# Decode attention with a Mish layer: wo loaded in runs of 32 KB, w1 read at unit step, the output made and stored as four rows

## The chip, the cores and the metric

The kernel runs on one core of a Trainium2 chip. A core has TensorE (matmuls into PSUM), VectorE, ScalarE, GpSimd, and SyncE (SP), which here issues most of the transfers; 16 DMA engines move data between the chip's memory and the core's 128-partition SBUF. The metric is the device time of one execution in microseconds. Three runs of the kernel before gave a median of 1329.84 us.

## The reference

One token (x of 512 elements) passes through an attention layer with a long cache and then a dense layer, each behind a layernorm and with its input added to its output. All tensors are bf16.

```python
# x (1,1,512); caches (1,32,32768,128); wq (512,4096); wo (4096,512)
# w1 (512,1376); b1 (1376); w2 (1376,512)
q = (layernorm(x) @ wq), as 32 heads of 128
scores = einsum("bhqd,bhkd->bhqk", q, k_cache) * 128 ** -0.5
o = einsum("bhqk,bhkd->bhqd", softmax(scores), v_cache)
h = x + o.reshape(1, 1, 4096) @ wo
g = layernorm(h) @ w1 + b1
out = h + (g * tanh(softplus(g))) @ w2
```

Each of the 32 heads reads 8 MB of keys and 8 MB of values, so the two caches are 512 MiB of the 548 MB that the kernel reads.

## The kernel before, in words

**A ring of six slots.** `ring` is a buffer of six slots, each 128 partitions x 32 KB, 4 MB in all. Everything large passes through it in the order of the list `order` (lines 186 to 193): wq, then the keys and values in halves of a head. The keys of head t + 1 alternate with the values of head t. After the values of head 30 come wo, then `w12` (w1 and w2 in one slot), then the two halves of the values of head 31. SP walks through this list (lines 231 to 255). Before an item it waits until the item six places earlier has been used up (line 234), and then it issues the transfers. The last item, the second half of head 31's values, is issued in four pieces of 64, 32, 16 and 16 tiles (`TAIL`), each with a semaphore of its own, so that work can begin on the first piece.

A half of keys or values is one transfer of 128 rows of 32 KB. wo is one transfer of 128 partitions x 32 heads x 1 KB (line 239): partition k receives, for each head h, row 128 h + k of wo. w1 is 128 rows of 11,008 B (line 241), w2 is 128 rows of 10,240 B and one last group of 96 rows of 1 KB (lines 242 and 243). Rows that are neighbours in memory lie in one partition: partition p holds rows 4p to 4p + 3 of w1.

**A half of keys** is 128 tiles of 128 x 128. TensorE transposes eight of them into PSUM (line 340), VectorE copies them to SBUF (line 343), and TensorE multiplies each by the query of the head (line 313). **A half of values** is 128 products of a tile with a column of probabilities, added up in PSUM (line 365). Between them stands the softmax of a head (lines 378 to 397). `oev` (line 373) divides a head's sum by its total and writes it as a column of `oT`.

**The end.** `project(h)` (line 431) multiplies the column of head h by the four column groups of wo. Here column group c holds the output elements 4m + c, m from 0 to 127, so `wo_v[:, h, c, :]` steps over four elements. Heads 0 to 30 are projected before the values of head 31 are used, head 31 after them. Then `lnh1` (line 445) adds x, `layernorm(1)` follows (lines 280 to 290), and 44 products make the hidden layer from w1 (line 457). Hidden element 10m + j stands in partition m of column j, so the weights step over ten elements; the last 96 hidden elements have a column of their own. The bias was put into the same PSUM columns earlier, by a product with the identity (line 439). Eight small steps make the activation (lines 461 to 467), 44 products with w2 make the output as a column of 128 x 4 (line 472), VectorE adds h (line 475), and SP stores 128 rows of 8 B (line 256).

**Order of work.** Each engine runs its own list in the order in which the program calls `S.step` for it; a step waits for the named steps of other engines. A transfer adds 16 to its semaphore, and `ready_wait` (line 201) gives the count at which an item has landed.

**The start.** x is loaded on ScalarE's queue (line 261) as 128 rows of 8 B and cast by VectorE (line 274); the two parts of b1 are loaded on GpSimd's queue (lines 266 and 268).

Of the kernel before, what the change touches and what calls it, by code (L numbers as in the profile page):

```python
# [6 lines left out]
BF16 = mybir.dt.bfloat16  # L7
F32 = mybir.dt.float32
I32 = mybir.dt.int32
ALU = mybir.AluOpType  # L10
# [3 lines left out]
PE, ACT, DVE, POOL, SP = "pe", "act", "dve", "pool", "sp"  # L14
# [81 lines left out]
def build_kernel(nc, A_x, A_k_cache, A_v_cache, A_wq, A_wo, B_w1, B_b1, B_w2, out):  # L96
    D = A_x.shape[-1]
    Dh = 128
    HD = A_wq.shape[1]
    H = HD // Dh  # L100
    Sk = A_k_cache.shape[2]
    F = B_w1.shape[1]
    KC = D // 128
# [5 lines left out]
    NS = 6  # L109
    TPS = 128  # L110
    SLOT = TPS * Dh
# [6 lines left out]
    FJ = F // 128  # L118
    FLAST = F - FJ * 128
    W1 = KC * F  # L120
    assert HALVES == 2 and KC == 4 and H <= 32 and FLAST > 0
    assert KC * HD == SLOT and H * D == SLOT
    assert W1 + (FJ + 1) * D <= SLOT

    allocs = []

    def sb(shape, dt, name):
        cm = nc.sbuf_tensor(name, shape, dt)
        t = cm.__enter__()
        allocs.append(cm)  # L130
        return t.ap()
# [7 lines left out]
    ring = sb([128, NS, SLOT], BF16, "ring")  # L139
# [3 lines left out]
    oT = sb([128, H], BF16, "oT")  # L143
# [3 lines left out]
    rtotc = sb([128, H], F32, "rtotc")  # L147
    gmax = sb([1, H], F32, "gmax")
    identi = sb([128, 128], I32, "identi")
    ident = sb([128, 128], F32, "ident")  # L150
    identb = sb([128, 128], BF16, "identb")
    onesm = sb([128, 128], F32, "onesmat")
    meanm = sb([128, 128], F32, "meanmat")
    epsc = sb([128, 1], F32, "epsc")
    xb = sb([128, KC], BF16, "xb")
    b1b = sb([128, FJ + 1], BF16, "b1b")
    b1f = sb([128, FJ + 1], F32, "b1f")
    lnx = sb([128, 2, 2, KC], F32, "lnx")
    lns = sb([128, 2, 8], F32, "lns")
    xnT = sb([128, 2, KC], BF16, "xnT")  # L160
    hsb = sb([128, 6, FJ + 1], F32, "hsb")
    actT = sb([128, FJ + 1], BF16, "actT")
    outT = sb([128, KC], BF16, "outT")

# [10 lines left out]
    hid_ps = S_b[0][:, 0:FJ + 1]  # L175
    y2_ps = S_b[1][:, 0:KC]

# [20 lines left out]
    def slot_of(what):  # L198
        return where[what] % NS

    def ready_wait(what):
        i = where[what]
        return (ready[i % NS], 16 * (i // NS + 1 + (2 if i % NS == where[("w12",)] % NS and i >= where[("w12",)] else 0)))

# [6 lines left out]
    wq_v = ring[:, slot_of(("wq",)), :].rearrange("p (k n) -> p k n", k=KC)  # L211
    wo_v = ring[:, slot_of(("wo",)), :].rearrange("p (h m c) -> p h c m", h=H, c=KC)
    w12 = ring[:, slot_of(("w12",)), :]
    w1_v = w12[:, 0:W1].rearrange("p (k n) -> p k n", k=KC)
    w2_v = w12[:, W1:W1 + FJ * D].rearrange("p (j m c) -> p j c m", j=FJ, c=KC)
    w2t_v = w12[0:FLAST, W1 + FJ * D:W1 + (FJ + 1) * D].rearrange("p (m c) -> p c m", c=KC)

    events = {}

    def program(S):  # L220
# [7 lines left out]
        def start(dst, src, s):  # L228
            S.dma(SP, lambda: sp.dma_start(dst, src).then_inc(s, 16))  # L229

        for i, what in enumerate(order):
            slot = i % NS
            if i >= NS:
                S.wait(SP, [free_name(order[i - NS])])
            flat = ring[:, slot, :]
            if what[0] == "wq":
                start(flat, A_wq.rearrange("(p k) n -> p (k n)", k=KC), ready[slot])
            elif what[0] == "wo":
                start(flat.rearrange("p (h n) -> p h n", h=H), A_wo.rearrange("(h k) n -> k h n", k=Dh), ready[slot])
            elif what[0] == "w12":  # L240
                start(w12[:, 0:W1], B_w1.rearrange("(p k) n -> p (k n)", k=KC), ready[slot])
                start(w12[:, W1:W1 + FJ * D], B_w2[0:FJ * 128, :].rearrange("(p j) n -> p (j n)", j=FJ), ready[slot])
                start(w12[0:FLAST, W1 + FJ * D:W1 + (FJ + 1) * D], B_w2[FJ * 128:F, :], ready[slot])
            else:
                kind, h, half = what
                cache = A_k_cache if kind == "k" else A_v_cache
                rows = cache[0, h, half * 128 * TPS:(half + 1) * 128 * TPS, :].rearrange("(p r) d -> p (r d)", r=TPS)
                if what == order[-1]:
                    at = 0
                    for n, s in zip(TAIL, piece_sems):  # L250
                        start(flat[:, at * Dh:(at + n) * Dh], rows[:, at * Dh:(at + n) * Dh], s)
                        at += n
                    assert at == TPS
                else:
                    start(flat, rows, ready[slot])
        S.dma(SP, lambda: sp.dma_start(out[0, 0, :].rearrange("(p c) -> p c", c=KC), outT[:, :]).then_inc(s_out, 16),
              waits=["fin"])
        S.wait(SP, [(s_out, 16)])


        S.dma(ACT, lambda: a.dma_start(xb[:, :], A_x[0, 0, :].rearrange("(p c) -> p c", c=KC)).then_inc(s_x, 16))
        if S.emit and S.only == ACT:
            a.preload_act_table_set("natural_log_exp_and_others")
        S.step(POOL, lambda: g.iota(identi[:, :], [[-1, 128]], base=0, channel_multiplier=1), name="iota")
        S.step(POOL, lambda: g.memset(b1b[:, :], 0.0), name="b1z")
        S.dma(POOL, lambda: g.dma_start(b1b[:, 0:FJ], B_b1[0:FJ * 128].rearrange("(p j) -> p j", j=FJ)).then_inc(s_b1, 16),
              waits=["b1z"])
        S.dma(POOL, lambda: g.dma_start(b1b[0:FLAST, FJ:FJ + 1], B_b1[FJ * 128:F].rearrange("(p o) -> p o", o=1)).then_inc(s_b1, 16))
        S.step(DVE, lambda: v.memset(onesm[:, :], 1.0), name="consts0")
# [3 lines left out]
        S.step(DVE, lambda: v.tensor_copy(identb[:, :], ident[:, :]), name="identb", waits=["ident"])  # L273
        S.step(DVE, lambda: v.tensor_copy(lnx[:, 0, 0, :], xb[:, :]), name="lnh0", waits=[(s_x, 16)])  # L274

# [96 lines left out]
        def oev(h):  # L372
            S.step(DVE, lambda: v.tensor_tensor(oT[:, h:h + 1], o_ps[:, h % 2:h % 2 + 1], rtotc[:, h:h + 1], ALU.mult),  # L373
                   name=f"oev{h}", waits=[f"pv{h}", f"rcp{h}"])

# [48 lines left out]

        def project(h):
            for c in range(KC):
                last = h == H - 1 and c == KC - 1
                waits = []
                if c == 0:
                    waits = [f"oev{h}"] + ([ready_wait(("wo",))] if h == 0 else [])  # L430
                S.step(PE, lambda c=c: t_.matmul(yps[:, c:c + 1], wo_v[:, h, c, :], oT[:, h:h + 1],  # L431
                                                 start=(h == 0 and c == 0), stop=last, skip_group_check=True),
                       name=("y" if last else None), waits=waits)

        for h in range(H - 1):
            project(h)
        soft_c(H - 1)
        S.step(DVE, lambda: v.tensor_copy(b1f[:, :], b1b[:, :]), name="b1f", waits=[(s_b1, 32)])
        S.step(PE, lambda: t_.matmul(hid_ps, ident[:, :], b1f[:, :], start=True, stop=False, skip_group_check=True),
               waits=["b1f", f"exp{H - 2}", f"exp{H - 1}"])  # L440
        pv(H - 1, 0, 0, TPS)
        pv(H - 1, 1, 0, TPS)
        oev(H - 1)
        project(H - 1)
        S.step(DVE, lambda: v.tensor_tensor(lnx[:, 1, 0, :], yps[:, 0:KC], lnx[:, 0, 0, :], ALU.add), name="lnh1", waits=["y"])
        layernorm(1)


        for j in range(FJ + 1):
            for kc in range(KC):  # L450
                if j < FJ:
                    w = w1_v[:, kc, 0:FJ * 128].rearrange("p (m j) -> p j m", j=FJ)[:, j, :]
                else:
                    w = w1_v[:, kc, FJ * 128:F]
                W = 128 if j < FJ else FLAST
                last = j == FJ and kc == KC - 1
                S.step(PE, lambda w=w, W=W, j=j, kc=kc, last=last: t_.matmul(  # L457
                    hid_ps[0:W, j:j + 1], w, xnT[:, 1, kc:kc + 1], start=False, stop=last, skip_group_check=True),
                    name=("hid" if last else None), waits=(["xn1", ready_wait(("w12",))] if j == 0 and kc == 0 else ()))
# [7 lines left out]
        S.step(DVE, lambda: v.tensor_tensor(actT[:, :], hid_ps, tt, ALU.mult), name="act", waits=["tt"])  # L467
        for c in range(KC):
            for j in range(FJ + 1):
                w = w2_v[:, j, c, :] if j < FJ else w2t_v[:, c, :]  # L470
                W = 128 if j < FJ else FLAST
                S.step(PE, lambda w=w, W=W, j=j, c=c: t_.matmul(y2_ps[:, c:c + 1], w, actT[0:W, j:j + 1],  # L472
                                                                start=(j == 0), stop=(j == FJ)),
                       name=("y2" if c == KC - 1 and j == FJ else None), waits=(["act"] if c == 0 and j == 0 else ()))
        S.step(DVE, lambda: v.tensor_tensor(outT[:, :], y2_ps, lnx[:, 1, 0, :], ALU.add), name="fin", waits=["y2"])

# [44 lines left out]
```

## Time and profile before

| what | us |
|---|---|
| median of three runs (lowest to highest) | 1329.84 (1328.77 to 1330.07) |
| the profiled execution, whole | 1330.19 |
| the span of its profile | 1328.4 |
| TensorE matmuls, busy | 1106.9 |
| VectorE, busy | 721.7 |
| ScalarE, busy | 20.6 |
| issue to landing, a half of keys (median) | 39.6 |
| issue to landing, wo | 43.5 |
| issue to landing, w1 | 39.1 |
| issue to landing, w2 without its last group | 9.2 |
| issue to landing, the output | 3.2 |

The span goes from the first to the last instruction of one profiled execution; its whole time is 1.8 us more. The mean granted clock of TensorE is 0.755 of full speed. Busy times of engines overlap. "Issue to landing" starts when SP issues a transfer, and holds the time behind other transfers in the queue. L343 and the like are lines of the kernel before.

### The profile page before, as it was taken

Reading aid. Unit: us, or ns where it says so; the run is one execution under the profiler, and the core shown is the slowest. Engines: PE = TensorE matmul, PEld = TensorE weight load, DVE = VectorE, ACT = ScalarE, POOL = GpSimd, SP = SyncE. Lnnn points to the kernel's source line nnn. Section 1 sums busy time; section 2 is a strip of 40 time slices with the busy share of each in tenths; the row PEclk is TensorE's granted clock in tenths of the full one; section 3 lists DMA queues with packets and bytes.
Section 4 is the critical chain, followed back from the end, with each engine's and each line's share of the span. In section 5 each row is a group of like instructions: output and inputs, shape, how many; then the busy total and the mean of one; then the engine's idle time right before and its main releaser. Section 6 shows DMA issues by size and latency. Waiting matters only on the chain.

```text
span 1328.4 us, 51752 instructions
## 1 busy us (share of the span) xinstructions
PE 1106.9 (83%) x25118; PEld 1073.6 (81%) x25118; DVE 721.7 (54%) x1210; ACT 20.6 (2%) x70; POOL 1.7 (0%) x8
## 2 busy tenths in 40 slices
PE   3887888988888988889889888888888988887984
PEld 3887887888887988888878888788887988887884
DVE  2754655655655654646556556556556555645540
ACT  0000000000000000000000000000000000000000
POOL 0000000000000000000000000000000000000000
PEclk9877868777878777667778667777778677768775
DMA  9999999999999999999999999999999999999974
GB/s 389 429 429 426 432 426 425 433 426 428 431 424 432 427 426 432 425 425 434 426 428 429 425 425 422 424 427 417 428 425 428 425 427 425 426 411 431 383 281 195
DMA packets 24080, 551.40 MB, mean 415 GB/s; under 512 B 2528, under 2 KB 6720, under 8 KB 6976
## 3 DMA queue, kind: packets, MB, share of 16 engines
q1 hardware_dynamic: 23664, 548.09, 96.9%
q8 instruction: 196, 3.21, 1.0%
q14 instruction: 12, 0.10, 0.0%
q10 hardware_dynamic: 144, 0.00, 0.0%
q0 software_dynamic: 64, 0.00, 0.0%
HBM read 548.08 MB, written 0.00 MB: 413 GB/s over the span
## 4 chain that ended last, share of the span: by engine, by line
PE 75%; issue 13%; DVE 8%; DMA 4%; SPq 0%; ACT 0%
PE tps L340 43%; PE ops L365 16%; PE sps L313 12%; DVE ering L343 7%; DMA ring<-in_A_v_cache_dram 2%; DMA ring<-in_A_k_cache_dram 2%; PE hlp L387 1%; PE hlp L382 1%; PE hlp L395 1%; PE sps L457 0%; SPq L229 0%; PE sps L472 0%; PE hlp L282 0%; DVE pmax L378 0%; ACT lns L287 0%
## 5 line engine op out<-in xcount | busy, mean ns | idle before, releaser
L343 DVE COPY ering<-tps 128x1024 bf16<-128x1024 bf16 x1024 | 681.7, 692 | 368.9 <-PE tps L340 365.9
L340 PE MATMUL tps<-identb,ring 128*128 128x128 bf16 x8192 | 755.7, 248 | 35.4 <-issue 31.7
L340 PEld LDWEIGHTS tps<-identb,ring 128*128 128x128 bf16 x8192 | 583.2, 112 | 42.6 <-issue 38.7
L313 PE MATMUL sps<-qT,ering 128*128 128x1 bf16 x8192 | 368.0, 166 | 39.9 <-issue 30.3
L313 PEld LDWEIGHTS sps<-qT,ering 128*128 128x128 bf16 x8192 | 340.4, 101 | 46.8 <-issue 33.5
L365 PE MATMUL ops<-pbuf,ring 128*128 128x1 bf16 x8192 | 236.7, 164 | 114.9 <-issue 106.3
L365 PEld LDWEIGHTS ops<-pbuf,ring 128*128 128x128 bf16 x8192 | 224.7, 101 | 131.6 <-issue 122.7
L373 DVE TENSOR_TENSOR oT<-ops,rtotc 128x1 bf16<-128x1 f32 x32 | 5.1, 161 | 93.5 <-PE ops L365 93.5
L384 DVE TENSOR_REDUCE gmax<-hlp 1x1 f32<-1x128 f32 x32 | 8.9, 279 | 77.2 <-PE hlp L382 77.2
L390 ACT ACTIVATE pbuf<-sps,nbias 128x256 bf16<-128x256 f32 x32 | 15.2, 474 | 1256.5 <-DVE nbias L389 1256.5
L378 DVE TENSOR_REDUCE pmax<-sps 128x1 f32<-128x256 f32 x32 | 13.6, 425 | 17.0 <-PE sps L313 17.0
L387 PE MATMUL hlp<-gmax,onesmat 1*128 1x1 f32 x64 | 18.7, 356 | 2.7 <-issue 2.3
L387 PEld LDWEIGHTS hlp<-gmax,onesmat 1*128 1x128 f32 x64 | 15.8, 303 | 3.7 <-issue 2.4
L382 PE MATMUL hlp<-ident,pmax 128*1 128x128 f32 x64 | 16.9, 357 | 1.7 <-issue 1.2
L282 PE MATMUL hlp<-lns,meanmat 128*128 128x2 f32 x4 | 1.2, 364 | 16.4 <-DVE lns L281 16.4
L282 PEld LDWEIGHTS hlp<-lns,meanmat 128*128 128x128 f32 x4 | 1.0, 313 | 16.5 <-DVE lns L281 16.5
L395 PE MATMUL hlp<-esum,onesmat 128*128 128x1 f32 x64 | 14.2, 292 | 0.0
L389 DVE TENSOR_SCALAR nbias<-hlp 128x1 f32<-128x1 f32 x32 | 5.1, 158 | 13.9 <-PE hlp L387 13.9
L395 PEld LDWEIGHTS hlp<-esum,onesmat 128*128 128x128 f32 x64 | 12.2, 239 | 0.0
L397 DVE RECIPROCAL rtotc<-hlp 128x1 f32<-128x1 f32 x32 | 5.2, 162 | 6.3 <-PE hlp L395 6.3
L274 DVE CAST lnx<-xb 128x4 f32<-128x4 bf16 x1 | 0.2, 171 | 13.6 <-DMA xb<-in_A_x_dram 13.6
L431 PE MATMUL yps<-oT,ring 128*128 128x1 bf16 x128 | 4.7, 172 | 1.9 <-issue 1.6
(43 smaller groups left out, 39.4 us busy)
## 6 DMA issues: line engine op xcount, KB each, us to landing
ring<-in_A_k_cache_dram SPq DMA_DIRECT2D x64, 4096.0 KB, 39.6
ring<-in_A_v_cache_dram SPq DMA_DIRECT2D x63, 4096.0 KB, 43.5
ring<-in_A_wq_dram SPq DMA_DIRECT2D x1, 4096.0 KB, 14.2
ring<-in_A_wo_dram SPq DMA_DIRECT2D x1, 4096.0 KB, 43.5
ring<-in_A_v_cache_dram SPq DMA_DIRECT2D x1, 2048.0 KB, 26.0
ring<-in_B_w_dram SPq DMA_DIRECT2D x1, 1376.0 KB, 39.1
ring<-in_B_w_dram SPq DMA_DIRECT2D x1, 1280.0 KB, 9.2
ring<-in_A_v_cache_dram SPq DMA_DIRECT2D x1, 1024.0 KB, 28.9
```

Source lines behind the costliest of these rows:

```text
L313: S.step(PE, lambda r=r: t_.matmul(S_b[h % 2][:, col0 + r:col0 + r + 1], ering[:, bg % NE, r, :], qT[:, h:h + 1], start=True, stop=True), ...
L340: S.step(PE, lambda r=r: t_.matmul(tb[:, r * 128:(r + 1) * 128], kt[:, gi * GT + r, :], identb[:, :], is_transpose=True, start=True, stop= ...
L343: S.step(DVE, lambda: v.tensor_copy(ering[:, bg % NE, :, :].rearrange("p r d -> p (r d)"), tb[:, :]), name=f"ev{bg}", waits=[f"trb{bg}"] + ...
L365: S.step(PE, lambda r=r, col=col: t_.matmul(o_ps[:, h % 2:h % 2 + 1], vt[:, r, :], pbuf[:, h % 2, col:col + 1], start=(col == 0), stop=(co ...
L373: S.step(DVE, lambda: v.tensor_tensor(oT[:, h:h + 1], o_ps[:, h % 2:h % 2 + 1], rtotc[:, h:h + 1], ALU.mult), name=f"oev{h}", waits=[f"pv{ ...
L378: S.step(DVE, lambda: v.tensor_reduce(pmax[:, h:h + 1], S_b[h % 2][:, 0:SCOLS], AXX, ALU.max), name=f"pmax{h}", waits=[f"qkh{h}"])
L382: S.step(PE, lambda: t_.matmul(A_REG, pmax[:, h:h + 1], ident[:, :], start=True, stop=True), name=f"A{h}", waits=[f"pmax{h}", "ident"])
L384: S.step(DVE, lambda: v.tensor_reduce(gmax[0:1, h:h + 1], A_REG, AXX, ALU.max), name=f"gmax{h}", waits=[f"A{h}"])
L387: S.step(PE, lambda: t_.matmul(B_REG, onesm[0:1, :], gmax[0:1, h:h + 1], start=True, stop=True), name=f"B{h}", waits=[f"gmax{h}", "consts0"])
L390: S.step(ACT, lambda: a.activation(pbuf[:, h % 2, :], S_b[h % 2][:, 0:SCOLS], ACTF.Exp, bias=nb[:, h:h + 1], scale=SC, accum_out=esum[:, h ...
L395: S.step(PE, lambda: t_.matmul(C_REG, onesm[:, :], esum[:, h:h + 1], start=True, stop=True), name=f"C{h}", waits=[f"exp{h}"])
L397: S.step(DVE, lambda: v.reciprocal(rtotc[:, h:h + 1], C_REG), name=f"rcp{h}", waits=[f"C{h}"])
```

## The change

wo is loaded in four transfers of 32 rows of 32 KB. Partition 32 b + h now holds rows 128 h + 32 b + j of wo for j = 0 to 31, so a block of 32 partitions holds the heads. `oT` is transposed in 32 x 32 blocks into `oX`, after which column j of `oX` matches column group j of wo in every partition. The products with wo go over j instead of over heads, with weights at unit step, and `y` comes in column groups of 128 consecutive elements. The last head isn't in `oX` (its column of `oT` is zero): its 128 rows of wo are loaded a second time, as a fourth transfer of `w12`, and `project_last` multiplies them by `oL`.

wq and w1 are loaded so that partition p of group k holds row 128 k + p; w2 so that group j holds 128 consecutive rows. The products with w1 have unit steps. x is loaded as four rows of 256 B, by SP and ahead of all else, and turned into columns by a product with the identity. b1 is loaded as 11 rows and put into PSUM by one bf16 product. The output is made as four rows of 128, in partitions 0, 32, 64 and 96: four f32 products with the identity put h there, and the products with w2 have the activation's column as the stationary operand and 128 columns of w2 as the moving one. VectorE copies all 128 partitions, and SP stores four rows of 256 B.

```diff
-    xb = sb([128, KC], BF16, "xb")
-    b1b = sb([128, FJ + 1], BF16, "b1b")
-    b1f = sb([128, FJ + 1], F32, "b1f")
-    outT = sb([128, KC], BF16, "outT")
+    oX = sb([128, H], BF16, "oX")
+    oL = sb([128, 1], BF16, "oL")
+    xr = sb([KC, 128], BF16, "xr")
+    b1r = sb([FJ + 1, 128], BF16, "b1r")
+    outr = sb([128, 128], BF16, "outr")
...
-    wo_v = ring[:, slot_of(("wo",)), :].rearrange("p (h m c) -> p h c m", h=H, c=KC)
+    wo_v = ring[:, slot_of(("wo",)), :].rearrange("p (j n) -> p j n", j=32)
...
-    w2_v = w12[:, W1:W1 + FJ * D].rearrange("p (j m c) -> p j c m", j=FJ, c=KC)
-    w2t_v = w12[0:FLAST, W1 + FJ * D:W1 + (FJ + 1) * D].rearrange("p (m c) -> p c m", c=KC)
+    w2_v = w12[:, W1:W2].rearrange("p (j n) -> p j n", j=FJ + 1)
+    wol_v = w12[:, W2:W2 + D]
...
+        start(xr[:, :], A_x[0, 0, :].rearrange("(c m) -> c m", c=KC), s_x)
...
-                start(flat, A_wq.rearrange("(p k) n -> p (k n)", k=KC), ready[slot])
+                start(wq_v, A_wq.rearrange("(k p) n -> p k n", k=KC), ready[slot])
             elif what[0] == "wo":
-                start(flat.rearrange("p (h n) -> p h n", h=H), A_wo.rearrange("(h k) n -> k h n", k=Dh), ready[slot])
+                for b in range(WB):
+                    start(flat[32 * b:32 * b + 32, :], A_wo.rearrange("(h b j) n -> b h (j n)", h=H, b=WB)[b], ready[slot])
             elif what[0] == "w12":
-                start(w12[:, 0:W1], B_w1.rearrange("(p k) n -> p (k n)", k=KC), ready[slot])
-                start(w12[:, W1:W1 + FJ * D], B_w2[0:FJ * 128, :].rearrange("(p j) n -> p (j n)", j=FJ), ready[slot])
-                start(w12[0:FLAST, W1 + FJ * D:W1 + (FJ + 1) * D], B_w2[FJ * 128:F, :], ready[slot])
+                start(w1_v, B_w1.rearrange("(k p) n -> p k n", k=KC), ready[slot])
+                start(w2_v[:, 0:FJ, :], B_w2[0:FJ * 128, :].rearrange("(j p) n -> p j n", j=FJ), ready[slot])
+                start(w2_v[0:FLAST, FJ, :], B_w2[FJ * 128:F, :], ready[slot])
+                start(wol_v, A_wo[(H - 1) * Dh:H * Dh, :], ready[slot])
...
-        S.dma(SP, lambda: sp.dma_start(out[0, 0, :].rearrange("(p c) -> p c", c=KC), outT[:, :]).then_inc(s_out, 16),
+        S.dma(SP, lambda: sp.dma_start(out[0, 0, :].rearrange("(c m) -> c m", c=KC), outr[0:128:32, :]).then_inc(s_out, 16),
...
-        S.step(DVE, lambda: v.tensor_copy(lnx[:, 0, 0, :], xb[:, :]), name="lnh0", waits=[(s_x, 16)])
+        S.step(PE, lambda: t_.matmul(X_REG, xr[:, :], identb[0:KC, 0:KC], start=True, stop=True), name="xT",
+               waits=["identb", (s_x, 16)])
+        S.step(DVE, lambda: v.tensor_copy(lnx[:, 0, 0, :], X_REG), name="lnh0", waits=["xT"])
...
+        def project(j):
             for c in range(KC):
+                first = j == 0 and c == 0
+                S.step(PE, lambda c=c, first=first: t_.matmul(
+                    yps[:, c:c + 1], wo_v[:, j, c * 128:(c + 1) * 128], oX[:, j:j + 1],
+                    start=first, stop=False, skip_group_check=True),
+                    waits=(["oX", ready_wait(("wo",))] if first else ()))
+
+        def project_last():
+            for c in range(KC):
+                S.step(PE, lambda c=c: t_.matmul(yps[:, c:c + 1], wol_v[:, c * 128:(c + 1) * 128], oL[:, :],
+                                                 start=False, stop=(c == KC - 1), skip_group_check=True),
+                       name=("y" if c == KC - 1 else None), waits=([f"oev{H - 1}", ready_wait(("w12",))] if c == 0 else ()))
+
+        S.step(DVE, lambda: v.transpose(oX[:, :], oT[:, :]), name="oX", waits=[f"oev{H - 2}", "oTz"])
+        for j in range(32):
+            project(j)
         soft_c(H - 1)
...
+        for c in range(KC):
+            S.step(PE, lambda c=c: t_.matmul(y2_ps[32 * c:32 * c + 1, :], lnx[:, 1, 0, c:c + 1], ident[:, :],
+                                             start=True, stop=False, skip_group_check=True),
+                   waits=(["lnh1", f"exp{H - 1}"] if c == 0 else ()))
...
-                    w = w1_v[:, kc, 0:FJ * 128].rearrange("p (m j) -> p j m", j=FJ)[:, j, :]
...
+                    hid_ps[0:W, j:j + 1], w1_v[:, kc, j * 128:j * 128 + W], xnT[:, 1, kc:kc + 1],
...
-        for c in range(KC):
-            for j in range(FJ + 1):
-                w = w2_v[:, j, c, :] if j < FJ else w2t_v[:, c, :]
...
+        for j in range(FJ + 1):
+            W = 128 if j < FJ else FLAST
+            for c in range(KC):
+                last = j == FJ and c == KC - 1
+                S.step(PE, lambda W=W, j=j, c=c: t_.matmul(
+                    y2_ps[32 * c:32 * c + 1, :], actT[0:W, j:j + 1], w2_v[0:W, j, c * 128:(c + 1) * 128],
+                    start=False, stop=(j == FJ), skip_group_check=True),
+                    name=("y2" if last else None), waits=(["act"] if j == 0 and c == 0 else ()))
-        S.step(DVE, lambda: v.tensor_tensor(outT[:, :], y2_ps, lnx[:, 1, 0, :], ALU.add), name="fin", waits=["y2"])
+        S.step(DVE, lambda: v.tensor_copy(outr[:, :], y2_ps), name="fin", waits=["y2"])
```

More of the change, by code (lines that the diff above doesn't have):

```diff
@@ L122, in build_kernel @@
     assert KC * HD == SLOT and H * D == SLOT
-    assert W1 + (FJ + 1) * D <= SLOT
+    W2 = W1 + (FJ + 1) * D
+    assert W2 + D <= SLOT
+    WB = Dh // 32
     allocs = []
@@ L175, in build_kernel @@
     hid_ps = S_b[0][:, 0:FJ + 1]
-    y2_ps = S_b[1][:, 0:KC]
+    X_REG = hlp[:, 204:204 + KC]
+    y2_ps = S_b[1][:, 0:128]
     sem = nc.alloc_semaphore
@@ L199, in slot_of, with extra_dmas @@
         return where[what] % NS
+    DMAS = {("wo",): WB, ("w12",): 4}
+    def extra_dmas(i):
+        return sum(n - 1 for w, n in DMAS.items() if where[w] <= i and (i - where[w]) % NS == 0)
     def ready_wait(what):
         i = where[what]
-        return (ready[i % NS], 16 * (i // NS + 1 + (2 if i % NS == where[("w12",)] % NS and i >= where[("w12",)] else 0)))
+        return (ready[i % NS], 16 * (i // NS + 1 + extra_dmas(i)))
     def free_name(what):
@@ L255, in program @@
                     start(flat, rows, ready[slot])
-        S.dma(SP, lambda: sp.dma_start(out[0, 0, :].rearrange("(p c) -> p c", c=KC), outT[:, :]).then_inc(s_out, 16),
+        S.dma(SP, lambda: sp.dma_start(out[0, 0, :].rearrange("(c m) -> c m", c=KC), outr[0:128:32, :]).then_inc(s_out, 16),
               waits=["fin"])
         S.wait(SP, [(s_out, 16)])
-        S.dma(ACT, lambda: a.dma_start(xb[:, :], A_x[0, 0, :].rearrange("(p c) -> p c", c=KC)).then_inc(s_x, 16))
         if S.emit and S.only == ACT:
@@ L264, in program @@
         S.step(POOL, lambda: g.iota(identi[:, :], [[-1, 128]], base=0, channel_multiplier=1), name="iota")
-        S.step(POOL, lambda: g.memset(b1b[:, :], 0.0), name="b1z")
-        S.dma(POOL, lambda: g.dma_start(b1b[:, 0:FJ], B_b1[0:FJ * 128].rearrange("(p j) -> p j", j=FJ)).then_inc(s_b1, 16),
+        S.step(POOL, lambda: g.memset(b1r[:, :], 0.0), name="b1z")
+        S.dma(POOL, lambda: g.dma_start(b1r[0:FJ, :], B_b1[0:FJ * 128].rearrange("(j p) -> j p", j=FJ)).then_inc(s_b1, 16),
               waits=["b1z"])
-        S.dma(POOL, lambda: g.dma_start(b1b[0:FLAST, FJ:FJ + 1], B_b1[FJ * 128:F].rearrange("(p o) -> p o", o=1)).then_inc(s_b1, 16))
+        S.dma(POOL, lambda: g.dma_start(b1r[FJ:FJ + 1, 0:FLAST], B_b1[FJ * 128:F].rearrange("(o p) -> o p", o=1)).then_inc(s_b1, 16))
+        S.step(DVE, lambda: v.memset(oT[:, :], 0.0), name="oTz")
         S.step(DVE, lambda: v.memset(onesm[:, :], 1.0), name="consts0")
@@ L372, in oev @@
         def oev(h):
-            S.step(DVE, lambda: v.tensor_tensor(oT[:, h:h + 1], o_ps[:, h % 2:h % 2 + 1], rtotc[:, h:h + 1], ALU.mult),
-                   name=f"oev{h}", waits=[f"pv{h}", f"rcp{h}"])
+            to = oT[:, h:h + 1] if h < H - 1 else oL[:, :]
+            S.step(DVE, lambda: v.tensor_tensor(to, o_ps[:, h % 2:h % 2 + 1], rtotc[:, h:h + 1], ALU.mult),
+                   name=f"oev{h}", waits=[f"pv{h}", f"rcp{h}"] + (["oTz"] if h == 0 else []))
         def soft_max(h):
@@ L422, in program @@
             soft_b(t + 1)
-        def project(h):
+        def project(j):
             for c in range(KC):
[L427 to L436, printed above, removed]
+                first = j == 0 and c == 0
[11 more added lines that the diff above has]
+            project(j)
         soft_c(H - 1)
-        S.step(DVE, lambda: v.tensor_copy(b1f[:, :], b1b[:, :]), name="b1f", waits=[(s_b1, 32)])
-        S.step(PE, lambda: t_.matmul(hid_ps, ident[:, :], b1f[:, :], start=True, stop=False, skip_group_check=True),
-               waits=["b1f", f"exp{H - 2}", f"exp{H - 1}"])
+        S.step(PE, lambda: t_.matmul(hid_ps, b1r[:, :], identb[0:FJ + 1, 0:FJ + 1], start=True, stop=False, skip_group_check=True),
+               waits=[(s_b1, 32), f"exp{H - 2}", f"exp{H - 1}"])
         pv(H - 1, 0, 0, TPS)
@@ L443, in program @@
         oev(H - 1)
-        project(H - 1)
+        project_last()
         S.step(DVE, lambda: v.tensor_tensor(lnx[:, 1, 0, :], yps[:, 0:KC], lnx[:, 0, 0, :], ALU.add), name="lnh1", waits=["y"])
         layernorm(1)
+        for c in range(KC):
+            S.step(PE, lambda c=c: t_.matmul(y2_ps[32 * c:32 * c + 1, :], lnx[:, 1, 0, c:c + 1], ident[:, :],
+                                             start=True, stop=False, skip_group_check=True),
+                   waits=(["lnh1", f"exp{H - 1}"] if c == 0 else ()))
         for j in range(FJ + 1):
             for kc in range(KC):
-                if j < FJ:
-                    w = w1_v[:, kc, 0:FJ * 128].rearrange("p (m j) -> p j m", j=FJ)[:, j, :]
-                else:
-                    w = w1_v[:, kc, FJ * 128:F]
                 W = 128 if j < FJ else FLAST
                 last = j == FJ and kc == KC - 1
-                S.step(PE, lambda w=w, W=W, j=j, kc=kc, last=last: t_.matmul(
-                    hid_ps[0:W, j:j + 1], w, xnT[:, 1, kc:kc + 1], start=False, stop=last, skip_group_check=True),
+                S.step(PE, lambda W=W, j=j, kc=kc, last=last: t_.matmul(
+                    hid_ps[0:W, j:j + 1], w1_v[:, kc, j * 128:j * 128 + W], xnT[:, 1, kc:kc + 1],
+                    start=False, stop=last, skip_group_check=True),
                     name=("hid" if last else None), waits=(["xn1", ready_wait(("w12",))] if j == 0 and kc == 0 else ()))
@@ L467, in program @@
         S.step(DVE, lambda: v.tensor_tensor(actT[:, :], hid_ps, tt, ALU.mult), name="act", waits=["tt"])
-        for c in range(KC):
-            for j in range(FJ + 1):
-                w = w2_v[:, j, c, :] if j < FJ else w2t_v[:, c, :]
[L471 to L475, printed above, removed]
+        for j in range(FJ + 1):
[7 more added lines that the diff above has]
+        S.step(DVE, lambda: v.tensor_copy(outr[:, :], y2_ps), name="fin", waits=["y2"])
     program(_Sched(nc, False, events, eng_sems))
```

## The prediction

> **What bounds the kernel now.** First the page's slices of the span, to see which resource is full, then the queues:
>
> ```profile
> PE   3887888988888988889889888888888988887984
> DMA  9999999999999999999999999999999999999974
> GB/s 389 429 429 426 432 426 425 433 426 428 431 424 432 427 426 432 425 425 434 426 428 429 425 425 422 424 427 417 428 425 428 425 427 425 426 411 431 383 281 195
> ...
> q1 hardware_dynamic: 23664, 548.09, 96.9%
> q8 instruction: 196, 3.21, 1.0%
> ```
>
> The DMA engines are full until about 1250 us and move some 428 GB/s; only the last three slices fall. TensorE is close to full too, so the second question is which of them waits at the end. TensorE's waits from 1240 us on:
>
> ```profile
> PE ops L365 <- DMA ring<-in_A_v_cache_dram: 8.5, 5, 5.6
> PE ops L365 <- issue: 4.7, 4, 1.6
> PE yps L431 <- issue: 1.6, 1, 1.6
> ```
>
> 8.5 us in five waits for the last head's values, the longest 5.6 us: TensorE has caught up there, and landings set the end. The third question is what the queue does before that, by the windows (the last three columns are TensorE's granted clock, the DMA engines' busy share and GB/s) and the timeline (start, length):
>
> ```profile
> 1250.00:1260.00 10.00, 9.72 (x123) 9.44 (x124) 5.85 (x11) 0.57 (x2) 0.00 (x0) 0.50 0.95 355
> 1260.00:1270.00 10.00, 8.41 (x233) 8.32 (x232) 5.36 (x9) 0.00 (x0) 0.00 (x0) 0.84 0.50 212
> 1270.00:1280.00 10.00, 9.26 (x163) 8.99 (x160) 5.25 (x8) 0.00 (x0) 0.00 (x0) 0.56 0.50 189
> ```
>
> ```profile
> 1249.95 32.32 SPq L229 DMA_DIRECT2D ring<-in_B_w_dram  x3
> ...
> 1318.51 2.82 PE L457 MATMUL sps<-xnT,ring 128*128 128x1 bf16 x44 [1.40 <-DVE xnT L290]
> 1322.92 1.62 PE L472 MATMUL sps<-actT,ring 128*128 128x1 bf16 x44 [1.59 <-DVE actT L467]
> 1324.58 0.16 DVE L475 TENSOR_TENSOR outT<-sps,lnx 128x4 bf16<-128x4 f32 x1 [1.71 <-PE sps L472]
> 1324.77 0.35 SPq L256 DMA_DIRECT2D out_dram<-outT  x1
> ```
>
> For 20 us the DMA share is 0.50: SP's issue of w1 is held for some 31 us behind the 4096 one-KB packets of wo. It looks like 10 us to be won. It isn't. The landing records (16 increments to a transfer, one from each DMA engine) split into two groups of eight. For the values v(30,1) eight engines land at 1246.0 to 1248.1 us and eight at 1273.0 to 1275.8; for wo 1257.9 to 1259.9 and 1283.9 to 1286.9. The gap grew from under 2 us in the first transfer to 28 us. The 196 instruction fetches of q8, 1.07 us each in the packet records, would on eight engines be 196 / 8 x 1.07 = 26 us for each, so I take the late eight to be those that also fetch instructions (an inference). The idle half is the leading eight. The late eight went from v(30,1) straight through wo (1275.83 to 1286.86, 11.03 us), w1 and w2 (to 1294.12), v(31,0) (to 1304.02) and the four pieces (to 1314.70). **The path is the late eight's packets, then 13.7 us of tail** (1314.70 to 1328.4). The hold costs them little: w1 and w2 took 7.26 us against 8 x 0.413 + 8 x 0.385 + 6 x 0.046 = 6.66 us by their packets.
>
> **The change, on the late eight.** The packet records give 1.213 us for 32 KB (27.0 GB/s for each engine, sixteen at once), 0.312 for 8 KB, 0.159 for 4 KB, 0.046 for 1 KB: bytes at 27.0 GB/s plus some 7 ns a packet.
> - x is now SP's first transfer, so wq and all behind it start one issue later: +0.40 us (SP's issue of wq took 0.38). x itself comes before wq, where it landed after it (15.12 against 14.94); the earlier queries gain nothing, because TensorE waits for the first keys until 24.6 us anyway.
> - wq in 8 KB rows: 32 x 0.312 - 8 x 1.213 = +0.28.
> - w1 in rows of 2752 B: 32 x (0.102 + 0.007) - 8 x 0.413 = +0.19. w2 in 1 KB rows: 80 x 0.046 - 8 x 0.385 = +0.60. The last head's rows of wo: 8 x 0.046 = +0.37.
> - wo: four transfers of 32 rows of 32 KB. Each engine still gets 8 packets, 2 from each. No row of the trace shows a transfer that goes to only 32 partitions. Low end, every engine keeps its rate: 8 x 1.213 = 9.70, so -1.33. High end, the 27.0 GB/s belong to the memory side and two engines meet on one path: the nearest row of sharing is a 32 KB packet that overlaps a 16 KB instruction packet on its engine and takes 1.68 to 1.76 us, 48 KB at about 28 GB/s, so a path shares its rate and does not add any. Then 2 x 9.70 = 19.41, +8.38. I take the high end: the steady 1.213 us of sixteen engines is seen only where each has its own 8 partitions, and now a quarter of the partitions gets all sixteen. That is a judgement; both ends stay in the range.
>
> [...]
>
> The stream: 0.40 + 0.28 + 0.19 + 0.60 + 0.37 = 1.84, with wo +10.22 (high) or +0.51 (low).
>
> What hides the rest: the transpose of o and the 128 products with wo (28 ns each at unit step, 3.6 us) come before TensorE's 5.6 us wait; if wo lands 8.4 us later, at about 1296, they end near 1301, and v(31,0) is then due near 1313. The products, the sum C of head 31, the bias product and the last value products are queued behind wo on TensorE, with over 10 us to spare. With wo short, the 5.6 us remain. SP's three more issues for wo and one for w12 (0.4 us each) run while the late eight have 30 us of packets queued. The bias is one product less in f32 and one DVE cast less, in the same wait.
>
> **The tail.** The granted clock is 0.50 from 1289 us to the end.
> - w1 at unit step: the 40 full products go from 58 ns apart to 28 (line 365 in the same stage: 128 in 3.57 us); the four of 96 columns stay at 80. 1.12 + 0.32 + 0.2 = 1.64 against 2.82: -1.2.
> - h put into the output by four f32 products of 1 x 128: line 382's pair takes 0.34 us at this clock, four 1.36, in the 1.40 us in which TensorE waits for the layernorm. I take 0, and +0.4 if half a product sticks out or delays line 457.
> - w2 now streams 128 columns past a one-column weight, to four groups of partitions. Nearest row: line 340, 128 columns, 107 ns apart at half clock (24 in 2.74 us): 44 x 0.107 + 0.2 = 4.9 against 1.62, +3.3. Low end, 28 ns each as in one-column products: 1.4, -0.2. I take +3.3, by the row with the same streamed width.
> - The last DVE step reads 128 columns of PSUM: line 378 (256 columns, 0.425 us) gives about 1 ns a column, so 0.29 against 0.16: +0.13.
> - The store: 4 packets of 256 B for 128 of 8 B. Of the sixteen engines the first landed at 1326.01, the fourth at 1326.25, the last at 1327.97. I take the fourth, -1.7; ends -1.96 and 0.
>
> [...]
>
> Tail: -1.2 + 0 + 3.3 + 0.13 - 1.7 = +0.5; ends -3.2 and +2.6.
>
> **Sum**: 10.22 + 0.5 = +10.7 on the span of 1328.4: 1339.1. That execution took 1330.19 in all, 0.35 over the median of 1329.84, so I add the difference to the median: **1340.5**. Its own range, with the ends of the tail and a wo that is only partly doubled: 1334 to 1345.
>
> **Rivals.** (1) *Each engine keeps its rate.* For it: 27.0 GB/s is constant whatever the load. Against: only one shape of transfer was seen. +0.51 + 0.5 = +1.0, 1330.8; with the tail's ends 1327.1 to 1332.9, mostly no change that can be told (0.2% is 2.66 us, about what a measurement of this kernel can tell).
> (2) *Faster: the output tail shortens.* Place: 1318.5 to 1328.4. The four rows of the output run side by side at 28 ns a product, and the store lands with its first engine: -3.2, and the 0.6 us that the held queue cost the late eight comes back: +0.51 - 3.2 - 0.6 = -3.3, 1326.5. It decides as long as wo's packets stay near 1.21 us; any sharing above 0.6 us in wo takes it back under 0.2%.
> (3) *The lead makes it worse.* The leading eight do wo some 28 us before the late eight, while these still read keys and values. If two leading engines put 128 KB each on the path of a late one, 256 KB at 27.0 GB/s are another 9.70 us: 1340.5 + 9.7 = 1350.2. Against: if the groups lie on separate paths, nothing crosses.
> That the change does not do what it says: the hold at 1250 us must go, since wo's 256 packets an engine become 8; w2's 80 may still hold SP for a while, which costs the late eight nothing.
>
> **Chances.** Forecast 0.53, (1) 0.18, (2) 0.14, (3) 0.15. So slower 0.69, counting a hundredth of (1), same 0.17, faster 0.14. The range for 8 in 10 must reach into (1) and (3): 1327 to 1352.
>
> **What would show it.** Right: 32 KB packets of wo at about 2.4 us, so fewer GB/s while they run; wo to the last engine some 19 us after v(30,1); TensorE's wait for v(31,0) over 10 us; line 457's group near 1.6 us; the store under 2 us. Wrong: wo's packets at 1.21 us, with the last landing within 2 us of 1314.7, or a late group whose keys before wo are themselves delayed (rival 3). The w2 group says which end of its term holds: 4.9 us or 1.4.

## The result, and the profile after

The changed kernel takes 1348.65 us (median of four runs, 1344.99 to 1349.4) against 1329.34 beside it; the ratio is 1.014, 95% interval 1.012 to 1.0159. It is slower by 1.4%. The profiled execution is the shortest of the four: 1344.99 us, with a span of 1343.2 against 1328.4 before. The accounts below are made on that span: they explain 14.8 us, while the medians lie 19.3 us apart; the longer runs have no profile.

First the page's slices, the counterpart of those shown of before:

```profile
DMA  9999999999999999999999999999999999999855
GB/s 401 424 431 425 426 432 424 430 431 426 426 431 424 429 428 431 426 430 427 427 428 429 426 430 428 429 425 430 427 429 426 431 426 429 424 425 399 245 171 238
...
q1 hardware_dynamic: 21680, 548.22, 96.7%
```

The bytes are nearly the same (548.09 MB before; 128 KB of wo are now loaded twice) and the packets fewer. The loss is in the last four slices. The windows of that stretch (start and end, length, busy time of TensorE's matmuls and weight loads, VectorE, ScalarE, GpSimd, each with its number of instructions; granted clock, DMA share, GB/s):

```profile
1240.00:1250.00 10.00, 2.73 (x68) 2.27 (x66) 0.59 (x3) 0.56 (x2) 0.00 (x0) 0.50 1.00 208
1250.00:1260.00 10.00, 8.48 (x163) 8.36 (x164) 7.42 (x12) 0.00 (x0) 0.00 (x0) 0.84 0.93 203
...
1280.00:1290.00 10.00, 7.79 (x156) 7.68 (x155) 6.70 (x10) 0.00 (x0) 0.00 (x0) 0.81 0.52 152
1290.00:1300.00 10.00, 6.06 (x128) 5.90 (x128) 3.88 (x6) 0.00 (x0) 0.00 (x0) 0.71 0.50 118
```

The first row is the one to learn from: from 1240 us on all sixteen DMA engines are busy (share 1.00) and move 208 GB/s, half of the usual rate of some 428. Here busy DMA engines are not fast ones. Two stretches are slow. Around 1240 to 1260 us the leading eight engines load wo while the late eight still load keys and values; from 1280 on the late eight finish head 30's values and load wo, and the leading eight idle (share 0.5): 152 and 118 GB/s, where eight engines alone moved 212 and 189 before. TensorE's waits from 1240 us on:

```profile
PE tps L354 <- DMA ring<-in_A_k_cache_dram: 14.6, 2, 7.5
PE ops L379 <- DMA ring<-in_A_v_cache_dram: 12.6, 4, 10.3
```

It now waits for keys too, which it did not do there before. The tail, by the timeline (start, length):

```profile
1242.26 63.22 SPq L238 DMA_DIRECT2D ring<-in_B_w_dram  x3
...
1334.84 0.61 PE L472 MATMUL sps<-ident,lnx 128*1 128x128 f32 x8
...
1336.30 1.54 PE L479 MATMUL sps<-xnT,ring 128*128 128x1 bf16 x44 [0.86 <-DVE xnT L304]
...
1339.44 1.34 PE L495 MATMUL sps<-ring,actT 128*1 128x128 bf16 x44 [1.59 <-DVE actT L490]
1340.83 0.29 DVE L499 CAST outr<-sps 128x128 bf16<-128x128 f32 x1 [1.45 <-PE sps L495]
1341.15 0.61 SPq L268 DMA_DIRECT2D out_dram<-outr  x1
```

The products with w1 fell from 2.82 to 1.54 us, those with w2 from 1.62 to 1.34, and SP's issues of w1 and w2 now hold it for 63 us, where the prediction had the hold of 32 us go, except for w2's part. The landing and packet records of both traces give the account of the late eight (times of the last of the sixteen landings):

| us | before | after |
|---|---|---|
| second half of head 30's values has landed | 1275.83 | 1289.51 |
| wo takes from there | 11.03 | 15.44 |
| w1, w2 (after: and the last head's rows) | 7.26 | 7.85 |
| v(31,0) and the four pieces | 20.58 | 19.72 |
| last landing | 1314.70 | 1332.52 |
| from there to the end | 13.7 | 10.7 |
| a 32 KB packet, usual | 1.213 | 1.213 |
| a 32 KB packet, 1240 to 1256 us (medians of stretches of 4 us) | 1.21 to 1.22 | 2.54 to 2.56 |

13.68 + 4.41 + 0.59 - 0.86 = 17.82 us later with the last landing, 3.0 us less behind it, 14.8 in all. These are the last of sixteen landings. The mean of the late eight's landings moves otherwise: head 30's values from 1274.48 to 1284.57, and from there to the mean of wo's last eight landings 11.2 us before and 18.1 after. So one late engine carries part of the first row's 13.68.

### The profile page after: what moved, and what is told of

It reads as the page before. It is cut to its first block, busy times and chain, and to the rows that moved or that the text cites. A ratio compares the mean times of both kernels' runs of the same rounds, so it can differ in the third digit from the quotient of the medians.

```text
span 1343.2 us, 51784 instructions
## 1 busy us (share of the span) xinstructions
PE 1098.2 (82%) x25130; PEld 1068.3 (80%) x25130; DVE 721.0 (54%) x1211; ACT 20.6 (2%) x70; POOL 1.7 (0%) x8
## 4 chain that ended last, share of the span: by engine, by line
PE 43%; DMA 42%; issue 6%; SPq 5%; DVE 4%; ACT 0%
DMA ring<-in_A_k_cache_dram 40%; PE tps L354 27%; PE sps L327 8%; PE ops L379 7%; SPq L238 5%; DVE ering L357 4%; DMA ring<-in_A_v_cache_dram 2%; PE hlp L402 1%; PE hlp L397 1%; PE hlp L410 0%; PE sps L479 0%; PE sps L495 0%; PE hlp L296 0%; DVE pmax L393 0%; ACT lns L301 0%
## 5 line engine op out<-in xcount | busy, mean ns | idle before, releaser
L405 ACT ACTIVATE pbuf<-sps,nbias 128x256 bf16<-128x256 f32 x32 | 15.1, 473 | 1282.5 <-DVE nbias L404 1282.5
L410 PE MATMUL hlp<-esum,onesmat 128*128 128x1 f32 x64 | 13.7, 283 | 0.0
L311 PE MATMUL hlp<-xnT,ring 128*128 128x1 bf16 x128 | 3.6, 165 | 10.1 <-DMA ring<-in_A_wq_dram 10.1
L311 PEld LDWEIGHTS hlp<-xnT,ring 128*128 128x128 bf16 x128 | 3.5, 104 | 10.2 <-issue 10.2
```

Source lines behind the costliest of these rows:

```text
L311: S.step(PE, lambda h=h, kc=kc: t_.matmul(Q_REG[:, h:h + 1], wq_v[:, kc, h * Dh:(h + 1) * Dh], xnT[:, 0, kc:kc + 1], start=(kc == 0), stop ...
L405: S.step(ACT, lambda: a.activation(pbuf[:, h % 2, :], S_b[h % 2][:, 0:SCOLS], ACTF.Exp, bias=nb[:, h:h + 1], scale=SC, accum_out=esum[:, h ...
L410: S.step(PE, lambda: t_.matmul(C_REG, onesm[:, :], esum[:, h:h + 1], start=True, stop=True), name=f"C{h}", waits=[f"exp{h}"])
```

## The experiments

Two explanations were open. **P, the paths**: a transfer to a block of 32 partitions makes two engines share one path. **H, the hold**: SP's issue is held longer, and the last values are issued late. Beside them stood the question whether the leading engines' wo also delays the late engines' keys and values (rival 3).

**1. wo contiguous, over all 128 partitions.**

```diff
-                for b in range(WB):
-                    start(flat[32 * b:32 * b + 32, :], A_wo.rearrange("(h b j) n -> b h (j n)", h=H, b=WB)[b], ready[slot])
+                start(flat, A_wo.rearrange("(p j) n -> p (j n)", j=32), ready[slot])
...
+        S.step(PE, lambda: t_.matmul(Q_REG, permb[:, :], oX[:, :], start=True, stop=True), name="oPp", waits=["oX", "perm"])
+        S.step(DVE, lambda: v.tensor_copy(oP[:, :], Q_REG), name="oP", waits=["oPp"])
...
-                    yps[:, c:c + 1], wo_v[:, j, c * 128:(c + 1) * 128], oX[:, j:j + 1],
+                    yps[:, c:c + 1], wo_v[:, j, c * 128:(c + 1) * 128], oP[:, j:j + 1],
```

> wo as one transfer of 128 rows of 32 KB (contiguous in memory: partition 4h+b holds rows 128h+32b+j), o brought to these partitions by one more product with a permuted identity and one more copy; all else as in the changed kernel. Theory P (a transfer to 32 partitions makes two DMA engines share one path, so its packets take twice as long): wo's packets at 1.21 us, keys and values before wo undisturbed, last landing near 1315 us of the span (1314.7 before, -1.3 for wo, +1.2 for smaller packets of w1, w2 and the last head's rows), tail 10.7 to 11 us, median near 1327 us, ratio 0.998. Theory H (the time is lost because SP's issue is held longer, 54 us against 31, and the last values are issued late): w2's 80 packets an engine are still there, SP is still held, time above 1338 us.

Measured: 1325.22 us (1325.1 to 1325.63), ratio 0.9958, interval 0.9945 to 0.997: faster than both kernels. Head 30's values land at 1274.44, wo takes 9.71 us, the last landing is at 1313.13, the tail 10.7. SP is held all the same, by the timeline:

```profile
1242.52 42.46 SPq L240 DMA_DIRECT2D ring<-in_B_w_dram  x3
```

That is longer than the 32.32 us before, in a faster kernel, so a long hold alone does not cost the time. It is shorter than the changed kernel's 63 us, though; what decides about H is experiment 2, where almost nothing is held. P stands, with 1.8 us less than the 1327 expected.

**2. The kernel before with only wo changed** to four transfers of 32 partitions (its rows then reach the products in another order).

```diff
-                start(flat.rearrange("p (h n) -> p h n", h=H), A_wo.rearrange("(h k) n -> k h n", k=Dh), ready[slot])
+                for b in range(4):
+                    start(flat[32 * b:32 * b + 32, :], A_wo.rearrange("(h b j) n -> b h (j n)", h=H, b=4)[b], ready[slot])
```

> The kernel before with one edit: wo in four transfers of 32 rows of 32 KB (the products with wo then read rows in another order than the reference's). w1 and w2 stay in 8 packets an engine, so SP is hardly held. Theory P: packets of 2.5 us, keys and values of head 30 delayed on the late engines, last landing near 1331, median near 1345 us. Theory H: no hold, so 1329 us or a little less.

Measured: 1354.05 us (1352.07 to 1355.38), ratio 1.0173 (1.0159 to 1.0187). The direction is P's, the size isn't: 9 us more than expected. Its timeline and a window say why:

```profile
1251.18 1.29 SPq L231 DMA_DIRECT2D ring<-in_B_w_dram  x3
1274.01 6.37 SPq L231 DMA_DIRECT2D ring<-in_A_v_cache_dram  x5
```

```profile
1284.00:1292.00 8.00, 6.90 (x127) 6.73 (x125) 5.01 (x9) 0.00 (x0) 0.00 (x0) 0.72 1.04 229
```

Almost nothing is held, and the kernel is the slowest of all: H falls. The leading eight have the last values to load while the late eight finish head 30's values and load wo: the share is full and the rate half. In those 8 us 16 KB packets (the first piece of the last values) take 1.23 us in the middle in place of 0.61. wo takes the late eight 20.9 us there, against 15.4 in the changed kernel, where the hold kept the leading eight idle (20.3 and 18.1 by the means of eight). So the hold was no loss; that it sheltered wo fits these numbers, but the two kernels differ in more than the hold.

**3. wo issued only when head 30's values have landed.**

```diff
             elif what[0] == "wo":
+                S.wait(SP, [ready_wait(("v", H - 2, HALVES - 1))])
                 for b in range(WB):
```

> The changed kernel with one wait more: SP issues wo only when the second half of head 30's values has landed on all engines, so that wo's packets meet no keys or values. Theory P with crossing (rival 3: the leading engines' wo packets also slow the late engines' keys and values): these values land near 1276 instead of 1289.5, wo follows with all sixteen engines sharing and takes 17 to 20 us, last landing near 1326, span near 1337, median 6 to 9 us below the changed kernel's 1348.65. Without crossing, the wait only adds a gap of some 2 us to the stream: 1349 us or more. Theory H: w12 and the last values are issued later still, time above 1350 us.

Measured: 1338.31 us (1337.91 to 1338.67), ratio 1.0055 (1.0042 to 1.0069), span 1336.8. Head 30's values land at 1274.23 on the late eight, not at 1289.51, and the last landing is at 1326.13. The windows:

```profile
1260.00:1270.00 10.00, 7.59 (x175) 7.51 (x175) 3.35 (x5) 0.00 (x0) 0.00 (x0) 0.66 0.51 218
...
1280.00:1290.00 10.00, 2.34 (x68) 2.04 (x66) 0.71 (x4) 0.56 (x2) 0.00 (x0) 0.60 1.02 211
```

Eight engines move 218 GB/s with keys and values; sixteen move 211 with wo. The four transfers land 5.0 us apart, at 2.55 us a packet: 2.1 times the usual price. A wait on the busiest queue made the kernel 10 us faster (6 to 9 were expected), because it kept two streams apart: the delay of the values ahead of wo is gone. Rival 3's crossing is shown.

**4. w2 in rows of 10 KB**, so that SP is held less (hidden elements then stand in another order).

```diff
-                start(w2_v[:, 0:FJ, :], B_w2[0:FJ * 128, :].rearrange("(j p) n -> p j n", j=FJ), ready[slot])
+                start(w2_v[:, 0:FJ, :], B_w2[0:FJ * 128, :].rearrange("(p j) n -> p j n", j=FJ), ready[slot])
```

> The changed kernel with w2 in rows of 10 KB as before (8 packets an engine in place of 80; hidden elements then stand in another order than the reference's). Theory P: the hold shrinks or goes, and the time falls by no more than 1 us: 1347 to 1349 us. Theory H: the time falls with the hold, by 10 us or more, to 1338 us or less.

Measured: 1351.48 us (1346.53 to 1352.84), ratio 1.0158 (1.0142 to 1.0173). The time is 2.5 us above the expected 1347 to 1349, but the interval overlaps that of the changed kernel. The timeline:

```profile
1242.45 21.61 SPq L238 DMA_DIRECT2D ring<-in_B_w_dram  x3
1264.10 10.84 SPq L238 DMA_DIRECT2D ring<-in_A_wo_dram  x1
1274.99 31.57 SPq L238 DMA_DIRECT2D ring<-in_A_v_cache_dram  x5
```

The issues of w1 and w2 hold SP for 21.6 us in place of 63, but the last head's rows of wo and the last values are then held in their turn, and SP is done at 1306.6 us, against 1309.5 in the changed kernel. So the hold moved more than it shrank, and this run says less about H than experiment 2. What it does show: the last values are issued from 1275 us on, some 31 us earlier, and nothing is won. They meet wo on the late eight, which takes 18.6 us.

**5. The transfers alone.** Rows of 32 KB from the key cache, 4 MB to a stage, no computation.

```diff
+    STAGES = [[(0, 128, 1)], [(0, 32, 1)] * 4, [(0, 64, 1)] * 2, [(32, 96, 1)] * 2,
+              [(0, 128, 4)] * 4, [(0, 128, 2)] * 2, [(0, 128, 1)]]
...
+                sp.dma_start(ring[a:b:step, n, :], rows[at:at + k, :]).then_inc(s, 16)
```

> Transfers alone, no computation (the output is zeros): rows of 32 KB from the key cache, 4 MB to a stage, each stage issued when the one before has landed. Stages: partitions 0-127 in one transfer; 0-31 four times; 0-63 twice; 32-95 twice; every fourth partition of 0-127 four times; every second twice; 0-127 again. [...] If what counts is only how many partitions a transfer has, 32-95 is as slow as 0-63 and every fourth as slow as 0-31.

The windows of the seven stages in this order; the columns are GpSimd's busy time, the clock, the DMA share and GB/s:

```profile
2.00:12.00 10.00, 0.00 (x0) 1.00 0.93 393
14.00:24.00 10.00, 0.00 (x0) 1.00 1.03 220
...
37.00:47.00 10.00, 0.00 (x0) 1.00 1.03 216
...
60.00:70.00 10.00, 0.00 (x0) 1.00 0.89 383
72.00:82.00 10.00, 0.00 (x0) 1.00 0.92 393
85.00:95.00 10.00, 0.00 (x0) 1.00 0.88 377
97.00:107.00 10.00, 0.00 (x0) 1.00 0.88 377
```

In this one run, partitions 0 to 31 take 2.56 us a packet (median), 0 to 63 the same 2.56, although they are twice as many. Partitions 32 to 95, also 64, take 1.213. So it isn't the count. That 0 to 31 and 32 to 63 share their paths and 64 to 95 have others fits these numbers; the paths themselves are not shown. Every fourth partition, 32 to a transfer, takes 1.213 as well, where the count alone would make it as slow as 0 to 31.

**6. Every fourth partition, in the kernel.** The contiguous version with four transfers again, each to partitions b, b + 4, b + 8 and so on.

```diff
-                start(flat, A_wo.rearrange("(p j) n -> p (j n)", j=32), ready[slot])
+                for b in range(WB):
+                    start(flat[b:128:WB, :], A_wo.rearrange("(h b j) n -> b h (j n)", h=H, b=WB)[b], ready[slot])
```

> The contiguous version with wo again in four transfers of 32 rows of 32 KB, the same memory rows to each as in the changed kernel, but to every fourth partition (b, b+4, b+8, ...) in place of a block of 32. The transfers alone ran at 1.21 us a packet in that shape. If which partitions a transfer reaches decides: packets of 1.21 us in the kernel too, nothing delayed before wo, time within 1 us of the contiguous version: 1325 to 1326.5 us. If four transfers of 32 rows cost by themselves, or the small share of 2 packets an engine: 1335 us or more.

Measured: 1325.15 us (1324.96 to 1325.53), ratio 0.9962 (0.9948 to 0.9976). The same four transfers of 32 rows from the same memory as in the changed kernel, and, by the two ratios, 1.8% less time (0.9962 / 1.014). Which partitions a transfer reaches at once is what decides.

**7. wo in rows of 1 KB**, as before the change, everything else changed (rows in another order).

```diff
-                for b in range(WB):
-                    start(flat[32 * b:32 * b + 32, :], A_wo.rearrange("(h b j) n -> b h (j n)", h=H, b=WB)[b], ready[slot])
+                start(flat.rearrange("p (h n) -> p h n", h=H), A_wo.rearrange("(h k) n -> k h n", k=Dh), ready[slot])
```

> The changed kernel with wo loaded as before, 128 partitions x 32 rows of 1 KB in one transfer (the products then read rows in another order than the reference's). Theory P: no sharing, wo 11.0 us on the late engines against 9.7 in the contiguous version; last landing near 1314.5, tail 10.7, 1.0 to 1.6 us above the contiguous version's 1325.22: 1326.2 to 1326.8 us. If the 1 KB packets and the hold cost more than their packets: above 1328 us.

Measured: 1327.08 us (ten runs, 1326.66 to 1327.43), ratio 0.9973 (0.9961 to 0.9986). wo takes 11.02 us from the landing of head 30's values, 1.31 more than in runs of 32 KB over all partitions, and the last landing is at 1314.26. The time is 0.3 us above the expected 1326.2 to 1326.8. So all of the change but the four transfers is worth 0.27%, and larger runs of wo another 1 to 2 us, if their partitions are chosen well: 1.31 us by the landings and 1.9 by the two medians, although the intervals of the two ratios overlap.

**8. The output in one row.** The contiguous version, the same products into one partition.

```diff
-    y2_ps = S_b[1][:, 0:128]
+    y2_ps = S_b[1][0:1, 0:D]
...
-                    y2_ps[32 * c:32 * c + 1, :], actT[0:W, j:j + 1], w2_v[0:W, j, c * 128:(c + 1) * 128],
+                    y2_ps[:, c * 128:(c + 1) * 128], actT[0:W, j:j + 1], w2_v[0:W, j, c * 128:(c + 1) * 128],
```

> The contiguous version with the output in one row of 512 in one partition instead of four rows in partitions 0, 32, 64 and 96: the same 44 products of 1 x 128 with w2 and four with the identity, now all in the same group of columns of the array; the last copy has 512 elements in one partition (about 0.7 us against 0.29), the store is one row of 1 KB. If the four groups ran side by side (the forecast's high end, 107 ns a product, holds for one group): products 4.7 to 4.9 us against 1.34, time near 1329.2 us. If a one-column weight makes each product short by itself: products 1.3 to 1.5 us, time near 1325.7 us.

Measured: 1328.93 us (1328.09 to 1329.22), ratio 0.9989 (0.9979 to 0.9999). Its timeline:

```profile
1315.42 1.86 PE L477 MATMUL sps<-ident,lnx 128*1 128x128 f32 x8
...
1317.22 1.54 PE L484 MATMUL sps<-xnT,ring 128*128 128x1 bf16 x44
...
1320.35 4.47 PE L500 MATMUL sps<-ring,actT 128*1 128x128 bf16 x44 [1.59 <-DVE actT L495]
```

In one group of partitions the 44 products take 4.47 us, in four 1.34 (3.3 times as fast, although the granted clock was 0.50 for the four groups and 0.56 on average for the one). The one-column weight did not make each product short by itself; the four groups ran side by side. The products with the identity take 1.86 in place of 0.61, last until 1317.28 and push the products with w1 back by about 0.3 us: what the forecast had as the upper bound of that term.

## Why the prediction was right, point by point

- **What bounds the kernel.** Right: landings on the late eight set the end, and the idle half of the engines at 1250 to 1280 us was not worth 10 us. Holds of 63 us (the changed kernel), 42.5, 1.3 and 21.6 (experiments 1, 2 and 4) go with 1348.65, 1325.22, 1354.05 and 1351.48: the time does not follow the hold. That the late eight are those that fetch instructions was an inference, and no run tests it.
- **wo's shared paths.** The high end was taken, and the price of a packet was nearly right: 2.55 us in experiment 3 against 2 x 1.213. The term of 19.41 us measured 15.44 from last landing to last landing, but 18.1 by the means of eight; where all sixteen load wo together (experiment 3) four times 5.0 us were measured, and with other traffic beside it 18.6 and 20.9 by last landings (experiments 4 and 2). The late eight slowed one another too: from 1290 to 1304 us, with the leading eight idle, their 32 KB packets took 2.18 us in the middle.
- **Crossing.** The step that failed is the sum, which gave the keys and values before wo nothing. Their last landing came 13.7 us later than before the change and 15.1 us later than in the contiguous version (1289.51 against 1275.83 and 1274.44). By the mean of the late eight it is 10.9 us against the contiguous version (1284.57 against 1273.65), so rival 3's price of 9.70 us was near. The rest sits on the last late engine, whose neighbours had landed shares of wo since 1286.1; that these slowed it is likely, not shown. Rival 3, which is the forecast with the crossing added and had a chance of 0.15, is what happened, and the sign named for it, a late group whose keys before wo are delayed, is there: 1350.2 against 1348.65 measured, where the forecast had 1340.5. In the three kernels that load wo in blocks of 32 while the two groups are apart (the changed one, experiments 2 and 4), the crossing came with the sharing.
- **What was luck.** The forecast added 10.2 us of stream and 0.5 of tail; the trace has 17.8 and -3.0. That the sum missed the profiled span by only 4.1 us (1339.1 against 1343.2) is in part luck: the shorter tail paid for nearly half of what the stream lacked. The range of 1327 to 1352 reached into the rivals and so did not tell them apart.
- **Signs.** Of those named for the forecast, these came: packets of 2.55 us, a wait of 10.3 us for v(31,0), 1.54 us for the products with w1, a store under 2 us. "Some 19 us after v(30,1)" for wo came as 15.44.
- **Small terms of the stream.** x ahead of wq and wq in 8 KB rows (0.68 us) can't be seen: head 30's values land at 1274.1 to 1274.4 in the five kernels that have both edits and leave these transfers undisturbed, against 1275.83. w1, w2 and the last head's rows were put at +1.16 on 7.26; they took +0.59 in the changed kernel, +1.24 in experiment 3 and +2.16 in the contiguous version (9.42 us).
- **The tail.** Forecast +0.5, measured -3.0. w1: 1.64 forecast, 1.54 measured. Last copy: 0.29 and 0.29. The store: its last engine lands 1.66 us after the issue, 3.20 before, so -1.54 against -1.7. The products with h are hidden, as said. The miss is w2, at 4.9 us by the row of line 340 and 1.34 in fact: that row is right for products into one group of partitions (4.47 us in experiment 8), but those into four overlapped and took 3.3 times less.
- **Rival 2** (a shorter output tail) was right about the tail, -3.0 against -3.2, and named the point from which it decides. With wo's packets at 1.21 us it is what happens: a ratio of 0.9958 in experiment 1.

What stays open: three of the four runs took 3.0 to 4.4 us more than the profiled one, and the kernels with crossing streams spread by 3.3 to 6.3 us, while the contiguous version stays within 0.5 and experiment 3 within 0.8. That the spread comes from where the two groups stand when they meet is likely, but only the shortest run of the changed kernel has a profile.

## What to carry to other kernels

Before you split a transfer by blocks of partitions, ask what each block costs; test it with the bare transfers and read share and GB/s together: here partitions 0 to 31 showed a share of 1.03 at 220 GB/s, all 128 a share of 0.93 at 393. The slow transfer also slowed what was in flight beside it here (head 30's values landed 13.7 us later), so price it on its neighbours too, and put that price into the sum and not into a rival. Where a split is needed, step the partitions: every fourth partition cost nothing here (1325.15 us against 1325.22), a block of 32 cost 1.8%.

## What the runs showed of the hardware that was not expected

- Transfers to every fourth partition ran at the same 27.0 GB/s an engine as those to all 128, although each has only 32 rows (1.213 us for 32 KB, experiment 5).
- A wait put on the transfer queue made the kernel faster by 10 us (1338.31 against 1348.65).
- One-row products into partitions 0, 32, 64 and 96 in turn took about a third of the time of the same products into one partition: 1.34 us for 44 at a granted clock of 0.50, against 4.47 at 0.56.
- The last 96 columns of w1 have weight loads of 96 columns, which stayed 80 ns apart where full ones at unit step were 27 apart (58 before the change, at a step of ten), at a granted clock of 0.50.
